# A fused spectral filter and gated GLU on one core: moments of six columns taken on ScalarE, transposed halves in PSUM banks of their own, first units of two weight slices

## Chip, core and metric

The kernel runs on one core of a Trainium2 chip. The metric is device time in microseconds (us). Engines: PE is TensorE (PEld its weight loads), DVE is VectorE, ACT is ScalarE, POOL is GpSimd, SP is SyncE, which issues most of the DMAs.

## What is computed

The input x has 2048 rows of 512 values in bf16. Each row is normalised over its 512 values. The normalised rows go two ways: through a 2-D real FFT, a product with a complex filter and the inverse FFT (part A), and through a gated GLU with 1792 hidden values (part B). The output is the sum of x and both parts.

```python
def _layernorm(x, axis=-1, eps=1e-5):
    m = jnp.mean(x, axis=axis, keepdims=True)
    v = jnp.var(x, axis=axis, keepdims=True)
    return (x - m) / jnp.sqrt(v + eps)
...
    X = rfft2(x) * (w_r + 1j * w_i); y = irfft2(X)            # A
...
    h = _gelu(x @ w_gate) * (x @ w_up); y = h @ w_down        # B
...
    return x + A(xn) + B(xn)          # xn = _layernorm(x)
```

## The kernel before

**Tiling.** The 2048 rows are cut into 16 groups that the code calls columns (c): row 16 p + c lies on partition p, column c. A column is a tile of 128 partitions by 512 values. The 512 values are four pieces of 128, numbered e. The 1792 hidden values are 14 slices of 128, numbered f; the weights Wg_sb and Wu_sb hold all slices in on-chip memory. Four columns form a block; there are four blocks, with transposed activations in the tiles xnT[0] to xnT[3].

**Stages.** For each column, VectorE takes mean and variance (bn_stats L396, bn_aggr L403), adds epsilon (L404), GpSimd raises to the power -0.5 (L406), and VectorE writes the normalised column xn (L412). Columns 0 to 3 are transposed by TensorE against an identity (L428) into PSUM and copied into xnT (L431): column 0 in two halves, the first copied by ScalarE and the second by VectorE, the others in one piece by ScalarE. Columns 4 to 15 are transposed by DMA (L437, issued by SP). The GLU (function glu) multiplies the transposed columns with slices of both weights (L502) into the PSUM tiles g_ps and u_ps, ScalarE applies gelu to g_ps (L519), and VectorE multiplies with u_ps into hT (L527). Two buffers each exist for g_ps and u_ps, so the matmuls of a unit wait for the gelu and the product of the unit two before. The list FIRST (L537) names the first units as (first column, number of columns, first slice, number of slices); then follow slices 6 to 13 for all four columns of block 0, then the other blocks.

The spectral part starts with folds of xn on VectorE (L555 to L567) and matmuls with the table RF_t (bp, L581); each of the four fold groups needs four normalised columns. Later stages (dp, ep, the filter, gp, yp) follow in the same style, and the last stage multiplies hT with w_down, adds the inverse transform in the same PSUM tile, adds x and stores.

**Loads.** x comes in five loads in this order of issue on SP, with the weight slices between them: column 0, column 1, columns 2 and 3, columns 4 to 7, columns 8 to 11; columns 12 to 15 and RF_t are issued later, behind the DMA transposes of columns 4 to 6.

**Order.** The order of instructions on each engine is not the order of the code. Every step is handed to a planner (class _Plan) with an engine, an estimated duration, dependencies, PSUM or work buffers, and a priority, mostly a due time. The planner runs a simple model (its own estimates for engines, DMA bandwidth and semaphore delay) and picks, whenever an engine is free in that model, the ready step with the lowest priority value. The order that comes out is written down and the engines run it as it stands. An engine's instructions therefore run in that order whether or not the model's times come true.

TensorE begins with ten matmuls on a constant tile (NWARM) and, behind column 0's transposes, four narrow ones (GAP).

Of the kernel before, what the change touches and what calls it, by code (L numbers as in the profile page):

```python
# [10 lines left out]
P = 128  # L11
BF16 = mybir.dt.bfloat16
# [206 lines left out]
def kernel(  # L219
# [43 lines left out]
    half = pc.tile([P, NC], F32, name="half")  # L263
    warm = pc.tile([P, D], BF16, name="warm")
    eps = pc.tile([P, 2], F32, name="eps")
    tiles = {}

    def cc(name):
# [43 lines left out]

    def load_x(c0, n, eng="SP", deps=()):
        q = nc.sync if eng == "SP" else nc.scalar
        o = load(n * P * D * 2, lambda: q.dma_start(out=x_t[:, c0:c0 + n], in_=x_v[:, c0:c0 + n]), deps, eng=eng)
        for c in range(c0, c0 + n):
            XD[c] = o

# [53 lines left out]
    o_mem = [add("POOL", 0.3, lambda: nc.gpsimd.memset(warm[:], 1.0), (), -20, lag=0.05),  # L372
             add("POOL", 0.2, lambda: nc.gpsimd.memset(half[:], -0.5), (), -15, lag=0.05)]  # L373
    wb = _Buf("S")
    NWARM, NGAP, GAP = 10, 1, 4

    def warm_mm(w):
        if "warm" not in tiles:
# [16 lines left out]
        tiles["st", c] = st  # L395
        V.bn_stats(out=st[:], in_=x_t[:, c])  # L396

    def layernorm(c0, n, due, after=(), halves=1):
        k = slice(c0, c0 + n)
        ag = []  # L400
        for c in range(c0, c0 + n):
            s = dve(0.6, lambda c=c: stats(c), [XD[c]] + list(after), due - 3.0 + 0.01 * (c - c0))
            ag.append(dve(0.15, lambda c=c: V.bn_aggr(out=mv[:, c], in_=tiles["st", c][:]), (s,), due - 3.2, ))  # L403
        e = dve(0.07, lambda: V.tensor_scalar(  # L404
            out=ve[:, k], in0=mv[:, k, 1], scalar1=EPS, scalar2=None, op0=ALU.add), ag, due - 5)
        r = add("POOL", 0.55, lambda: nc.gpsimd.tensor_tensor(  # L406
            out=rstd[:, k], in0=ve[:, k], in1=half[:, k], op=ALU.pow), (e, o_mem[1]), due - 5, lag=0.1)
        for c in range(c0, c0 + n):
            XN[c] = []
            for h in range(halves):  # L410
                d = slice(h * D // halves, (h + 1) * D // halves)
                XN[c].append(dve(0.04 + 0.29 / halves, lambda c=c, d=d: V.tensor_scalar(  # L412
                    out=xn[:, c, d], in0=x_t[:, c, d], scalar1=mv[:, c, 0:1], scalar2=rstd[:, c:c + 1],
                    op0=ALU.subtract, op1=ALU.mult), (r,), due - 2.5))
        return ag

    def pe_transpose(c, due):
        XT[c] = []
        b = _Buf("S")
        n = len(XN[c])  # L420
        for h in range(n):
            es = range(h * NE // n, (h + 1) * NE // n)

            def mm(h=h, es=es):
                if h == 0:
                    psum(f"tp.{c}", [P, NE, P], BF16)
                for e in es:
                    nc.tensor.transpose(tiles[f"tp.{c}"][:, e], xn[:, c, e * P:(e + 1) * P], ident)  # L428

            def ev(es=es, eng=(nc.scalar.copy, V.tensor_copy)[h]):  # L430
                eng(out=xnT[c // 4][:, es[0]:es[-1] + 1, c % 4], in_=tiles[f"tp.{c}"][:, es[0]:es[-1] + 1])  # L431

            o = pe(0.24 / n, mm, (XN[c][h], d_ident), due - 2, new=(b,) if h == 0 else (), use=(b,))
            XT[c].append((act, dve)[h](0.1 + 0.35 / n, ev, (o,), due - 30, use=(b,)))

    def dma_transpose(c, due):
        XT[c] = [dma(320e3, lambda: nc.sync.dma_start_transpose(out=xnT[c // 4][:, :, c % 4], in_=xn[:, c]),  # L437
                    XN[c], due - 30, lag=1.0)]

    first = layernorm(0, 1, -28, (), 2)  # L440
    layernorm(1, 1, -25, first)
    for c in range(4):
        if c == 2:
            layernorm(2, 2, -22, XT[0])
        pe_transpose(c, -28 + 3 * c)
        if c < NGAP:
            dummies(GAP, -29.9 + 3 * c, XN[c], P)
    for c0, n, due in ((4, 2, 14), (6, 2, 16), (8, 4, 24), (12, 4, 32)):
        layernorm(c0, n, due)
        for c in range(c0, c0 + n):  # L450
            dma_transpose(c, due)
        if c0 == 6:
            d_rf = load(P * NC * P * 2, lambda: nc.sync.dma_start(
                out=RF_t[:], in_=rf_d.rearrange("p (c k) -> p c k", c=NC)), XN[7])
            load_x(12, 4, deps=XN[7])
# [30 lines left out]
    def glu(c0, n, f0, nf=1, extra=()):  # L486
        sb, o, w = c0 // 4, (c0 % 4) * P, n * P
        gb, ub, eb = _Buf("G"), _Buf("U"), _Buf("ge")
        key = f"{c0}.{n}.{f0}"
        t = now[0]  # L490
        dur = NE * (w / 2400.0 + 0.0024)
        now[0] += 2 * dur * nf + 0.2

        def rhs(e):
            return xnT[sb][:, e, c0 % 4:c0 % 4 + n, :].rearrange("p c q -> p (c q)")

        def mm(nm, W, tag, a, b):
            if a == 0:
                psum(f"{nm}.{key}", [P, D], tag=tag)
            for f in range(a, b):  # L500
                for e in range(NE):
                    nc.tensor.matmul(tiles[f"{nm}.{key}"][:, f * w:f * w + w], lhsT=W[:, e, (f0 + f) * P:(f0 + f + 1) * P],  # L502
                                     rhs=rhs(e), start=(f + e == 0), stop=(f == nf - 1 and e == NE - 1),
                                     skip_group_check=nf > 1)

        g = [o for c in range(c0, c0 + n) for o in XT[c]]
        step = min(nf, 2)
        us = []
        for a in range(0, nf, step):
            deps = g[-1:] if a else g  # L510
            new = [([], []), ([gb], [ub])][a == 0]
            g = [pe(step * dur, lambda a=a: mm("g_ps", Wg_sb, "G", a, a + step), deps + [WD[f0 + a][0]], t,
                    new=new[0], use=(gb,))]
            us = [pe(step * dur, lambda a=a: mm("u_ps", Wu_sb, "U", a, a + step), us + g + [WD[f0 + a][1]], t,
                     new=new[1], use=(ub,))]

        def ge():
            e = work(f"ge.{key}", [P, D], "ge")
            nc.scalar.activation(out=e[:, 0:nf * w], in_=tiles[f"g_ps.{key}"][:, 0:nf * w], func=AF.Gelu_apprx_tanh)  # L519

        a = act(0.1 + nf * w / 1200.0, ge, g, t - 40, new=(eb,), use=(gb,))

        def mul():
            out = hslot(sb, f0)[:, o:o + w]
            if nf > 1:
                out = tiles["hT", sb][:, f0:f0 + nf, o:o + w]
            V.tensor_tensor(out=out, in0=tiles[f"u_ps.{key}"][:, 0:nf * w].rearrange("p (f w) -> p f w", w=w)  # L527
                            if nf > 1 else tiles[f"u_ps.{key}"][:, 0:w],
                            in1=tiles[f"ge.{key}"][:, 0:nf * w].rearrange("p (f w) -> p f w", w=w)
                            if nf > 1 else tiles[f"ge.{key}"][:, 0:w], op=ALU.mult)  # L530

        h = dve(0.08 + nf * w / 960.0, mul, us + [a] + list(extra), t - 40, use=(ub, eb))
        for c in range(c0, c0 + n):
            HT.setdefault(c, []).append(h)
        return h

    FIRST = [(0, 1, 0, 4), (1, 1, 0, 4), (0, 2, 4, 2), (2, 2, 0, 2), (2, 2, 2, 2), (2, 2, 4, 2)]  # L537
    for c, n, f, nf in FIRST + [(0, 4, f, 1) for f in range(6, NFC)]:
        glu(c, n, f, nf)

# [386 lines left out]
```

## Time and profile before

| | us |
|---|---|
| median of 8 runs | 179.66 (179.37 to 180.81) |
| the profiled execution | 179.58 |
| its span | 177.8 |
| PE busy | 172.9 (97%) |
| DVE busy | 118.3 (67%) |
| ACT busy | 87.5 (49%) |
| POOL busy | 18.5 (10%) |
| gelu, 128 x 512 (L519), mean of one | 0.598 |
| product into hT, 128 x 512 (L527), mean of one | 0.686 |
| bn_stats, 128 x 512 (L396), mean of one | 0.678 |

The span is the time from the first to the last instruction in the trace; the time of an execution also has what lies around it, here 1.8 us. Every time below is counted from the start of the span. PE's busy time counts pipelined matmuls whose ends are modelled, so a rate is read from the distance between the starts of two groups rather than from their durations. In a row of a timeline the brackets say how long the engine was idle before the instruction and what released it.

### The profile page before, as it was taken

How to read it: one execution, taken by the hardware profiler on the slowest of the kernel's cores; microseconds unless marked ns; L12 is line 12 of the kernel's file. 1: busy time of each engine (PE TensorE's matmuls, PEld its weight loads, DVE VectorE, ACT ScalarE, POOL GpSimd, SP SyncE). 2: the span in 40 equal slices, each digit the busy share in tenths (PEclk: the TensorE clock that was granted, in tenths of full speed). 3: DMA queues.
4: the chain of work that ended last, by engine and by line, in shares of the span. 5: the costliest groups of instructions: out<-in, count | busy, mean ns of one | idle time of the engine just before them, and what ended most of it. 6: DMA issues, size and time to landing. Idle time of an engine off the chain costs nothing.

```text
span 177.8 us, 3041 instructions
## 1 busy us (share of the span) xinstructions
PE 172.9 (97%) x1100; PEld 92.6 (52%) x1100; DVE 118.3 (67%) x266; ACT 87.5 (49%) x158; POOL 18.5 (10%) x33
## 2 busy tenths in 40 slices
PE   6899999999999999999999999999999999999993
PEld 2598545545554554554555455555445444544463
DVE  2759999999537995889999885336442541632522
ACT  3262427456789737999998855453111211211100
POOL 3212128743300000000000000000000000000000
PEclk9999999999999999999999999999999999999999
DMA  5999379899498001402211122000222221322212
GB/s 135 311 354 366 84 238 116 219 293 174 76 346 262 0 0 24 97 2 59 61 42 39 41 59 49 16 0 0 79 72 73 76 89 59 92 78 70 71 47 59
DMA packets 23182, 19.24 MB, mean 108 GB/s; under 512 B 8512, under 2 KB 21824, under 8 KB 23168
## 3 DMA queue, kind: packets, MB, share of 16 engines
q1 hardware_dynamic: 22176, 17.57, 35.9%
q0 software_dynamic: 320, 1.19, 3.1%
q10 hardware_dynamic: 672, 0.30, 0.6%
q8 instruction: 8, 0.13, 0.3%
q14 instruction: 6, 0.05, 0.1%
HBM read 13.28 MB, written 2.10 MB: 86 GB/s over the span
## 4 chain that ended last, share of the span: by engine, by line
PE 87%; ACT 3%; DMA 3%; DVE 3%; SPq 1%; issue 1%; DVEq 0%
PE u_ps L502 25%; PE g_ps L502 24%; DMA Wu_sb<-in_B_w_up_dram 3%; ACT E L652 2%; PE yp L818 2%; PE bp L581 2%; PE gp L767 2%; PE yp__2078 L872 2%; PE yp__2052 L872 2%; PE yp__2025 L872 2%; PE yp__1994 L872 2%; PE yp__1967 L872 2%; PE yp__1878 L872 2%; PE yp__1851 L872 2%; PE yp__1820 L872 2%; PE yp__1793 L872 2%
## 5 line engine op out<-in xcount | busy, mean ns | idle before, releaser
L502 PE MATMUL g_ps<-xnT,Wg_sb 128*128 128x512 bf16 (+2 forms) x264 | 58.1, 347 | 0.4 <-ACT xnT L431 0.2
L502 PE MATMUL u_ps<-xnT,Wu_sb 128*128 128x512 bf16 (+2 forms) x264 | 57.9, 347 | 0.3 <-DMA Wu_sb<-in_B_w_up_dram 0.3
L527 DVE TENSOR_TENSOR hT<-u_ps,ge 128x512 bf16<-128x512 f32 x56 | 38.4, 686 | 17.7 <-PE u_ps L502 15.1
L519 ACT ACTIVATE ge<-g_ps 128x512 bf16<-128x512 f32 x56 | 33.5, 598 | 30.9 <-PE g_ps L502 28.2
L502 PEld LDWEIGHTS <-Wu_sb 128*128 128x128 bf16 x264 | 24.3, 98 | 22.5 <-DMA Wu_sb<-in_B_w_up_dram 0.5
L502 PEld LDWEIGHTS <-Wg_sb 128*128 128x128 bf16 x264 | 24.1, 98 | 21.2 <-issue 0.4
L872 PEld LDWEIGHTS <-hT 128*128 128x128 bf16 x252 | 23.0, 98 | 21.9
L824 ACT CAST yf<-yp 128x512 bf16<-128x512 f32 x16 | 9.3, 586 | 37.6 <-PE yp L818 37.6
L652 ACT CAST E<-ep 64x512 bf16<-64x512 f32 x32 | 18.5, 579 | 1.1 <-PE ep L646 0.7
L396 DVE BATCH_NORM_STATS2 st<-x_t 128x6 f32<-128x512 bf16 x16 | 10.5, 678 | 4.7 <-DMA x_t<-in_A_x_dram 4.6
L629 ACT CAST ds<-dp 128x512 bf16<-128x512 f32 x16 | 8.8, 589 | 1.1 <-PE dp L624 1.0
L773 ACT CAST Gs<-gp 128x512 bf16<-128x512 f32 x16 | 8.6, 593 | 1.0 <-PE gp L767 1.0
L406 POOL TENSOR_TENSOR rstd<-ve,half 128x2 f32<-128x2 f32 (+2 forms) x7 | 6.6, 947 | 22.1 <-DVE ve L404 22.1
L585 ACT CAST Bs<-bp 128x512 bf16<-128x512 f32 x16 | 8.3, 603 | 0.5 <-PE bp L581 0.5
L818 PEld LDWEIGHTS <-Gs 128*128 128x128 bf16 x64 | 4.8, 98 | 3.5
L412 DVE TENSOR_SCALAR xn<-x_t,mv,rstd 128x512 bf16<-128x512 bf16 (+1 forms) x17 | 6.1, 400 | 0.3 <-POOL rstd L406 0.3
L818 PE MATMUL yp<-CT,Gs 128*128 128x128 bf16 x64 | 6.0, 219 | 0.0
L380 PE MATMUL warm<-warm 128*128 128x512 bf16 (+1 forms) x14 | 4.7, 502 | 1.3 <-POOL half L373 1.3
L683 DVE TENSOR_TENSOR m<-X,TW 128x1024 bf16<-128x1024 bf16 x8 | 5.5, 693 | 0.2
L624 PEld LDWEIGHTS <-Bs 128*128 128x128 bf16 x64 | 4.4, 98 | 2.4
L689 DVE TENSOR_TENSOR m<-X,TW 128x1024 bf16<-128x1024 bf16 x8 | 5.5, 685 | 0.0
L646 PE MATMUL ep<-ds,CT 128*128 128x512 bf16 x16 | 5.4, 379 | 0.0
(103 smaller groups left out, 168.8 us busy)
## 6 DMA issues: line engine op xcount, KB each, us to landing
y<-in_A_x_dram SPq DMA_DIRECT2D x16, 128.0 KB, 2.2
F<-F SPq DMA_DIRECT2D x32, 64.0 KB, 2.0
out_dram<-y SPq DMA_DIRECT2D x15, 128.0 KB, 1.7
Wd_sb<-in_B_w_down_dram SPq DMA_DIRECT2D x2, 896.0 KB, 7.3
x_t<-in_A_x_dram SPq DMA_DIRECT2D x3, 512.0 KB, 6.8
Wg_sb<-in_B_w_gate_dram SPq DMA_DIRECT2D x2, 512.0 KB, 6.8
Wu_sb<-in_B_w_up_dram SPq DMA_DIRECT2D x2, 512.0 KB, 9.1
Wg_sb<-in_B_w_gate_dram SPq DMA_DIRECT2D x3, 256.0 KB, 4.5
```

The lines of the kernel that those rows point to most:

```text
L396: V.bn_stats(out=st[:], in_=x_t[:, c])
L406: r = add("POOL", 0.55, lambda: nc.gpsimd.tensor_tensor(out=rstd[:, k], in0=ve[:, k], in1=half[:, k], op=ALU.pow), (e, o_mem[1]), due - 5, ...
L502: nc.tensor.matmul(tiles[f"{nm}.{key}"][:, f * w:f * w + w], lhsT=W[:, e, (f0 + f) * P:(f0 + f + 1) * P], rhs=rhs(e), start=(f + e == 0), ...
L519: nc.scalar.activation(out=e[:, 0:nf * w], in_=tiles[f"g_ps.{key}"][:, 0:nf * w], func=AF.Gelu_apprx_tanh)
L527: V.tensor_tensor(out=out, in0=tiles[f"u_ps.{key}"][:, 0:nf * w].rearrange("p (f w) -> p f w", w=w) if nf > 1 else tiles[f"u_ps.{key}"][:, ...
L585: nc.scalar.copy(out=o, in_=tiles[f"bp.{cg}.{q}"][:].rearrange("p c (r g a) -> p (c r) g a", r=2, a=4))
L629: nc.scalar.copy(out=ds[:].rearrange("p (s k t) -> p s k t", s=2, t=2), in_=tiles[f"dp.{G}"][:].rearrange("p s t k -> p s k t"))
L652: nc.scalar.copy(out=tiles[f"E.{g}"][64 * h:64 * h + 64, r], in_=tiles[f"ep.{g}.{h}"][64 * r:64 * r + 64])
L773: nc.scalar.copy(out=o, in_=tiles[f"gp.{g}.{h}"][:].rearrange("p q (n a) -> p (q n) a", a=4))
L818: nc.tensor.matmul(yp[:, q], lhsT=tiles["G"][:, q, c], rhs=IQ[q], start=(q == 0), stop=(q == 3), skip_group_check=True)
L824: nc.scalar.copy(out=tiles[f"yf.{c // 2}"][:, c % 2], in_=tiles[f"yp.{c}"][:])
L872: nc.tensor.matmul(y[:, s], lhsT=tiles[sb, f][:, cl * P:(cl + 1) * P], rhs=Wd_sb[:, f, s], start=(f == 0), stop=False)
```

## The change

ScalarE takes the moments of columns 1, 3, 5, 7, 9 and 11 with two ACTIVATE instructions that accumulate along the row: Identity with scale -1/512 gives the negative mean, and Square with that as bias gives 512 times the variance. Their elementwise outputs go to xn and are overwritten. For these columns VectorE scales and adds epsilon in one instruction and normalises with an addition in place of a subtraction. Epsilon is now added for each column by itself; the power still runs for a group of columns. Columns 2 and 3 become groups of their own.

Column 1 is also normalised and transposed in two halves, and each half has its own PSUM tile. Inside a GLU unit the matmuls with the first two pieces e come before those with the last two. FIRST starts with two slices for column 0 and two for column 1, and slices 2 and 3 are done for both columns together. Two of the four narrow fillers go. The planner is told half the bytes for the loads of columns 0 and 1, and columns 4 to 15 are made to depend on column 3's normalised values (in the planner alone). All of this is run through the planner again, so the order on every engine changes.

```diff
--- before.py
+++ after.py
@@ -263,6 +263,7 @@
     half = pc.tile([P, NC], F32, name="half")
     warm = pc.tile([P, D], BF16, name="warm")
     eps = pc.tile([P, 2], F32, name="eps")
+    sm = pc.tile([P, 2, NC], F32, name="sm")
     tiles = {}
 
     def cc(name):
@@ -312,7 +313,7 @@
 
     def load_x(c0, n, eng="SP", deps=()):
         q = nc.sync if eng == "SP" else nc.scalar
-        o = load(n * P * D * 2, lambda: q.dma_start(out=x_t[:, c0:c0 + n], in_=x_v[:, c0:c0 + n]), deps, eng=eng)
+        o = load(n * P * D * (2 if c0 > 1 else 1), lambda: q.dma_start(out=x_t[:, c0:c0 + n], in_=x_v[:, c0:c0 + n]), deps, eng=eng)
         for c in range(c0, c0 + n):
             XD[c] = o
 
@@ -372,7 +373,7 @@
     o_mem = [add("POOL", 0.3, lambda: nc.gpsimd.memset(warm[:], 1.0), (), -20, lag=0.05),
              add("POOL", 0.2, lambda: nc.gpsimd.memset(half[:], -0.5), (), -15, lag=0.05)]
     wb = _Buf("S")
-    NWARM, NGAP, GAP = 10, 1, 4
+    NWARM, NGAP, GAP = 10, 1, 2
 
     def warm_mm(w):
         if "warm" not in tiles:
@@ -395,58 +396,70 @@
         tiles["st", c] = st
         V.bn_stats(out=st[:], in_=x_t[:, c])
 
-    def layernorm(c0, n, due, after=(), halves=1):
+    def layernorm(c0, n, due, after=(), halves=1, acts=(), after2=()):
         k = slice(c0, c0 + n)
-        ag = []
+        es = []
         for c in range(c0, c0 + n):
-            s = dve(0.6, lambda c=c: stats(c), [XD[c]] + list(after), due - 3.0 + 0.01 * (c - c0))
-            ag.append(dve(0.15, lambda c=c: V.bn_aggr(out=mv[:, c], in_=tiles["st", c][:]), (s,), due - 3.2, ))
-        e = dve(0.07, lambda: V.tensor_scalar(
-            out=ve[:, k], in0=mv[:, k, 1], scalar1=EPS, scalar2=None, op0=ALU.add), ag, due - 5)
+            if c in acts:
+                m = act(0.62, lambda c=c: moment(c, AF.Identity, scale=-1.0 / D, accum_out=sm[:, 0, c:c + 1]),
+                        [XD[c]] + list(after), due - 30)
+                q = act(0.72, lambda c=c: moment(c, AF.Square, bias=sm[:, 0, c:c + 1], scale=1.0,
+                                                 accum_out=sm[:, 1, c:c + 1]), [m] + list(after2), due - 30)
+                es.append(dve(0.07, lambda c=c: V.tensor_scalar(
+                    out=ve[:, c:c + 1], in0=sm[:, 1, c:c + 1], scalar1=1.0 / D, scalar2=EPS, op0=ALU.mult, op1=ALU.add),
+                    (q,), due - 9))
+            else:
+                s = dve(0.6, lambda c=c: stats(c), [XD[c]] + list(after), due - 3.0 + 0.01 * (c - c0))
+                a = dve(0.15, lambda c=c: V.bn_aggr(out=mv[:, c], in_=tiles["st", c][:]), (s,), due - 3.2)
+                es.append(dve(0.07, lambda c=c: V.tensor_scalar(
+                    out=ve[:, c:c + 1], in0=mv[:, c, 1:2], scalar1=EPS, scalar2=None, op0=ALU.add), (a,), due - 5))
         r = add("POOL", 0.55, lambda: nc.gpsimd.tensor_tensor(
-            out=rstd[:, k], in0=ve[:, k], in1=half[:, k], op=ALU.pow), (e, o_mem[1]), due - 5, lag=0.1)
+            out=rstd[:, k], in0=ve[:, k], in1=half[:, k], op=ALU.pow), es + [o_mem[1]], due - 5, lag=0.1)
         for c in range(c0, c0 + n):
             XN[c] = []
+            mean, op = (sm[:, 0, c:c + 1], ALU.add) if c in acts else (mv[:, c, 0:1], ALU.subtract)
             for h in range(halves):
                 d = slice(h * D // halves, (h + 1) * D // halves)
-                XN[c].append(dve(0.04 + 0.29 / halves, lambda c=c, d=d: V.tensor_scalar(
-                    out=xn[:, c, d], in0=x_t[:, c, d], scalar1=mv[:, c, 0:1], scalar2=rstd[:, c:c + 1],
-                    op0=ALU.subtract, op1=ALU.mult), (r,), due - 2.5))
-        return ag
+                XN[c].append(dve(0.04 + 0.29 / halves, lambda c=c, d=d, mean=mean, op=op: V.tensor_scalar(
+                    out=xn[:, c, d], in0=x_t[:, c, d], scalar1=mean, scalar2=rstd[:, c:c + 1],
+                    op0=op, op1=ALU.mult), (r,), due - 2.5))
+
+    def moment(c, func, **kw):
+        nc.scalar.activation(out=xn[:, c], in_=x_t[:, c], func=func, **kw)
 
     def pe_transpose(c, due):
         XT[c] = []
-        b = _Buf("S")
         n = len(XN[c])
         for h in range(n):
+            b = _Buf("S")
             es = range(h * NE // n, (h + 1) * NE // n)
 
             def mm(h=h, es=es):
-                if h == 0:
-                    psum(f"tp.{c}", [P, NE, P], BF16)
+                psum(f"tp.{c}.{h}", [P, NE, P], BF16)
                 for e in es:
-                    nc.tensor.transpose(tiles[f"tp.{c}"][:, e], xn[:, c, e * P:(e + 1) * P], ident)
-
-            def ev(es=es, eng=(nc.scalar.copy, V.tensor_copy)[h]):
-                eng(out=xnT[c // 4][:, es[0]:es[-1] + 1, c % 4], in_=tiles[f"tp.{c}"][:, es[0]:es[-1] + 1])
-
-            o = pe(0.24 / n, mm, (XN[c][h], d_ident), due - 2, new=(b,) if h == 0 else (), use=(b,))
+                    nc.tensor.transpose(tiles[f"tp.{c}.{h}"][:, e], xn[:, c, e * P:(e + 1) * P], ident)
+
+            def ev(h=h, es=es, eng=(nc.scalar.copy, V.tensor_copy)[h]):
+                eng(out=xnT[c // 4][:, es[0]:es[-1] + 1, c % 4], in_=tiles[f"tp.{c}.{h}"][:, es[0]:es[-1] + 1])
+
+            o = pe(0.24 / n, mm, (XN[c][h], d_ident), due - 2, new=(b,))
             XT[c].append((act, dve)[h](0.1 + 0.35 / n, ev, (o,), due - 30, use=(b,)))
 
     def dma_transpose(c, due):
         XT[c] = [dma(320e3, lambda: nc.sync.dma_start_transpose(out=xnT[c // 4][:, :, c % 4], in_=xn[:, c]),
                     XN[c], due - 30, lag=1.0)]
 
-    first = layernorm(0, 1, -28, (), 2)
-    layernorm(1, 1, -25, first)
-    for c in range(4):
-        if c == 2:
-            layernorm(2, 2, -22, XT[0])
-        pe_transpose(c, -28 + 3 * c)
-        if c < NGAP:
-            dummies(GAP, -29.9 + 3 * c, XN[c], P)
+    layernorm(0, 1, -28, (), 2)
+    layernorm(1, 1, -25, (), 2, (1,))
+    pe_transpose(0, -28)
+    dummies(GAP, -29.9, XN[0], P)
+    pe_transpose(1, -25)
+    layernorm(2, 1, -22, XN[1])
+    pe_transpose(2, -22)
+    layernorm(3, 1, -19, XT[0], 1, (3,), XT[1])
+    pe_transpose(3, -19)
     for c0, n, due in ((4, 2, 14), (6, 2, 16), (8, 4, 24), (12, 4, 32)):
-        layernorm(c0, n, due)
+        layernorm(c0, n, due, XN[3], 1, (5, 7, 9, 11))
         for c in range(c0, c0 + n):
             dma_transpose(c, due)
         if c0 == 6:
@@ -497,11 +510,10 @@
         def mm(nm, W, tag, a, b):
             if a == 0:
                 psum(f"{nm}.{key}", [P, D], tag=tag)
-            for f in range(a, b):
-                for e in range(NE):
-                    nc.tensor.matmul(tiles[f"{nm}.{key}"][:, f * w:f * w + w], lhsT=W[:, e, (f0 + f) * P:(f0 + f + 1) * P],
-                                     rhs=rhs(e), start=(f + e == 0), stop=(f == nf - 1 and e == NE - 1),
-                                     skip_group_check=nf > 1)
+            for f, e in sorted(((f, e) for f in range(a, b) for e in range(NE)), key=lambda k: (k[1] // 2, k)):
+                nc.tensor.matmul(tiles[f"{nm}.{key}"][:, f * w:f * w + w], lhsT=W[:, e, (f0 + f) * P:(f0 + f + 1) * P],
+                                 rhs=rhs(e), start=(f + e == 0), stop=(f == nf - 1 and e == NE - 1),
+                                 skip_group_check=nf > 1)
 
         g = [o for c in range(c0, c0 + n) for o in XT[c]]
         step = min(nf, 2)
@@ -534,7 +546,7 @@
             HT.setdefault(c, []).append(h)
         return h
 
-    FIRST = [(0, 1, 0, 4), (1, 1, 0, 4), (0, 2, 4, 2), (2, 2, 0, 2), (2, 2, 2, 2), (2, 2, 4, 2)]
+    FIRST = [(0, 1, 0, 2), (1, 1, 0, 2), (0, 2, 2, 2), (0, 2, 4, 2), (2, 2, 0, 2), (2, 2, 2, 2), (2, 2, 4, 2)]
     for c, n, f, nf in FIRST + [(0, 4, f, 1) for f in range(6, NFC)]:
         glu(c, n, f, nf)
```

## Prediction

> **What bounds the kernel now.** I began with the busy line of the page, then the waits of the matmul queue.
>
> ```profile
> PE 172.9 (97%) x1100; PEld 92.6 (52%) x1100; DVE 118.3 (67%) x266; ACT 87.5 (49%) x158; POOL 18.5 (10%) x33
> ...
> PE warm L380 <- POOL half L373: 1.3, 1, 1.3
> PE u_ps L502 <- DMA Wu_sb<-in_B_w_up_dram: 0.3, 1, 0.3
> PE g_ps L502 <- ACT xnT L431: 0.2, 1, 0.2
> ```
>
> TensorE is busy for 172.9 of 177.8 us, and its three named waits all fall before 9.1 us. The table of stretches gives 40.00 busy in 100 to 140 us and 39.88 in 60 to 100. So from 9.03 us on, TensorE is the bound, and whatever the change gives or takes must show as an idle stretch of that engine: a little can be won before 9 us, anything can be lost after. The next rows are timelines (start, duration, engine, line, operation), of PE, ACT and DVE in turn.
>
> ```profile
> 9.03 0.62 PE L502 MATMUL u_ps<-xnT,Wu_sb 128*128 128x128 bf16 x8 [0.28 <-DMA Wu_sb<-in_B_w_up_dram]
> ...
> 11.72 1.04 PE L502 MATMUL g_ps<-xnT,Wg_sb 128*128 128x256 bf16 x8
> 12.59 1.04 PE L502 MATMUL u_ps<-xnT,Wu_sb 128*128 128x256 bf16 x8
> 13.46 1.04 PE L502 MATMUL g_ps<-xnT,Wg_sb 128*128 128x256 bf16 x8
> ...
> 27.34 1.06 PE L581 MATMUL bp<-RF_t,xf 128*128 128x128 bf16 x16
> ...
> 11.70 1.07 ACT L431 COPY xnT<-tp 128x512 bf16<-128x512 bf16 x2
> 12.79 0.60 ACT L519 ACTIVATE ge<-g_ps 128x512 bf16<-128x512 f32 x1
> ...
> 7.24 1.29 DVE L396 BATCH_NORM_STATS2 st<-x_t 128x6 f32<-128x512 bf16 x2
> ...
> 12.42 0.69 DVE L396 BATCH_NORM_STATS2 st<-x_t 128x6 f32<-128x512 bf16 x1 [1.32 <-DMA x_t<-in_A_x_dram]
> 13.03 0.67 DVE L527 TENSOR_TENSOR hT<-u_ps,ge 128x512 bf16<-128x512 f32 x1
> ```
>
> Starts tell the rate better than durations: eight matmuls of 128 columns take 0.45 us, eight of 256 take 0.875, four of 512 take 0.865, sixteen bp 0.89. The matmul at 13.46 is the first to use columns 2 and 3; ScalarE copied their transposes at 11.70, so they had some 0.7 us in hand. VectorE sat idle for 1.32 us until columns 4 to 7 of x landed at 12.42. ScalarE has no wait for a load of x at all. That is what changes.
>
> **Part 1, TensorE's own work.** Two of four filler matmuls go: 2 x 0.055 = 0.11. Eight groups of 0.45 (3.58 us) become four of 0.45 and two of 0.875 (3.54). Together 0.15 us less. Sorting matmuls by half of the contraction moves none across a group.
>
> **Part 2, the first 11.7 us.** Now the first copy of column 0 at 6.08 waits for all four transposes (the last ends at 6.05), and VectorE's copy waits for ScalarE's. With a bank each, ScalarE can copy once two transposes are done, at 5.82, and the first matmul can go at 6.2 instead of 6.51. Against that, the second half of column 0 stands on VectorE behind column 1's variance, which waits for ScalarE's two passes: x1 landed at 1.19 + 2.9 = 4.1, Identity to 4.7, Square to 5.45, so that half starts at 5.6 rather than 5.4.
>
> Then the built order of ScalarE matters. After the copy of column 0 it has Identity of column 3, then the first gelu, then column 1's copy. Columns 2 and 3 land at 2.13 + 5.1 = 7.23 us, as VectorE's row at 7.24 agrees. Identity at 7.26, one pitch of 0.49 (the second of the two copies at 11.70 adds 0.48), a gelu of 256 elements some 0.30, and column 1's copy runs 8.05 to 8.42. Its matmuls start at 8.48 and go through: u 8.93, the 256-wide group 9.38 and 10.25, transposes of 2 and 3 at 11.13, next group at 11.57 instead of 11.72. Weights are in time (the slice that arrives at 9.03 is now wanted at 10.25). Column 3's Square ends at 9.05, its normalised column at 10.65, before 11.13. So the bank split and the reordered start, which could save up to 1.3 us if nothing waited, give only the 0.15 of part 1.
>
> **Part 3, the wait that is added.** The next Identity on ScalarE is column 5's, which needs the same load for which VectorE waited until 12.42. Behind it in ScalarE's queue stand **the two copies of columns 2 and 3**, then Square of column 5 and the gelu of the running group. Now these copies start at 11.70; in the change they start one pitch after 12.42: 12.42 + 0.49 + 0.48 + 0.59 = 13.98 for the end of the second, and 0.06 to the matmul (6.45 to 6.51 in the first copy): **14.04 against 13.46**, when TensorE alone would be ready at 11.57 + 1.75 = 13.32. Loss 0.58 after the gain of 0.15 is used up.
>
> An accumulating ACTIVATE has no row here. Lower bound: the gelu's 0.60 and pitch 0.49. Upper: no overlap and 0.2 more, 0.8, which makes it 14.35. I take the gelu's row. The Trainium skill ("ScalarE: Activation LUTs", section What ACT_TABLE_LOAD costs) gives 186 ns + 0.833 ns an element, 93 ns more for a per-partition bias, 93 ns of overlap: 0.61 and 0.71, pitch 0.52, so by the rule 14.07. The same page (Rules for kernel authors) says additions and multiplications belong on VectorE, not ScalarE. Rows: statistics of a column cost VectorE 0.69 + 0.18, and here two passes on ScalarE, 0.60 + 0.71. As throughput this is hidden: ScalarE is busy 1.96 of 4 us from 12 to 16, and 12 passes add some 7 us over 4 to 21 us. By the rule alone one would book ScalarE's longer work, by the rows nothing; my loss comes from where the passes stand in the queue.
>
> **Part 4, from 14 to 24 us.** Does the crowded ScalarE hold TensorE again? Gelu of (columns 0-1, slices 4-5) ends at 15.1, wanted at 15.8; of (columns 2-3, slices 0-1) 16.1, wanted 17.5. Column 9's Identity waits for columns 8 to 11 (8.38 + 9.0 = 17.38), with the gelu behind it ending at 18.5, wanted at 19.3. VectorE's product of (columns 0-1, slices 4-5) ends at 16.4, wanted at 16.7, the tightest. VectorE loses six statistics and aggregations (about 6 x 0.7 by pitch) and gains nine small variance instructions (9 x 0.08). POOL gets one more power, 0.6, beside TensorE. Nothing stalls, by 0.3 us at least.
>
> **Part 5, the fold matmuls.** The built order puts the first bp group two units earlier: after three units at 256 columns and three at 512, so at 14.04 + 6 x 0.875 + 6 x 0.865 = 24.48 (the same sum with ten groups gives 27.36 now, as the trace has it). It needs RF_t, behind three transposes on SP:
>
> ```profile
> 17.98 4.35 SPq L437 DMA_TRANSPOSE xnT<-xn  x3
> 22.38 0.57 SPq L453 DMA_DIRECT2D RF_t<-spec_rf  x1
> ...
> DMA to landing us min/median/max: 4.2/4.2/4.2
> ```
>
> (The last line is RF_t's alone.) It landed at 26.6, 0.75 us before its use. In the change column 4 is normalised by 16.8 (after the product at 15.75 to 16.4); the three transposes issue for 1.3, 1.2 and 1.2 us at 16.85, 18.25 and 19.5; RF_t issues at 20.75 and lands at **24.95**. TensorE waits **0.47**. Bounds: none, if the load takes 3.7; 1.0, if column 4 or 6 slips by half a us.
>
> **Part 6, the rest.** The order of later groups differs, but each load and spectral step moves up some 3 us with its consumer. The second fold group, due near 30.2, has its operand at 28.7; the first gp group, due at 72.7, its F near 68. I cost this at nothing; the cover is VectorE's lighter load, and if it fails, one late product or F costs 0.3 to 1.
>
> **Sum.** 0.58 + 0.47 = 1.05 on the profiled execution's 179.58 us (span 177.8 and 1.8 around it): 180.63; the median of the runs shown, 179.66, is within 0.1. **Forecast 180.6 us.**
>
> **The clock.** Removing fillers could hurt otherwise. The ten warm-up matmuls of 512 columns follow each other at 0.43 us, later ones at 0.216. "TensorE: Matmul & The Clock Gate" (Part 1) says half rate returns after an idle window of about 3.4 us. My longest idle stretch is 0.8 (7.7 to 8.5), so by the rule nothing; yet little work lies between 5.5 and 9 us. If a window fell to half rate, 3.4 us would do 1.7 us of work, less 0.7 hidden before 14.04: 1.0 more, 181.6.
>
> **Rivals.**
> - Only ScalarE's wait counts, RF_t is in time: 180.16. For: 0.47 is small beside the spread of load times (x between 2.5 and 9.0 us). Against: the transposes' issue chain is firm. 0.25.
> - Both waits and a third loss (dear accumulation, a late product, the half clock): 181.1 to 182. For: thin covers in part 4. 0.18.
> - Faster or no change: column 5's pass does not hold the copies. This decides if columns 4 to 7 land before 13.32 - 0.06 - 0.59 - 0.48 - 0.49 = 11.70 us; then the 0.15 of part 1 stays, 179.43, and, should columns 2 and 3 also land early, up to 1.3, 178.3. Against: loads keep their order, and VectorE's row puts the landing at 12.42. RF_t would have to be early as well. 0.10, about half beyond 0.3%.
> - The forecast, both waits: 0.47, 180.3 to 181.0.
>
> **Chances and range.** A measurement of this kernel tells 0.3%, 0.54 us, from no change, so the edge is 180.2. Slower takes the forecast, the third-loss case and a third or so of the first rival: 0.74. The rest of that rival and half the fast case: within, 0.21. Faster 0.05. Range 179.9 to 181.6: from a cheap first wait to the half clock.
>
> **What would show it.** In the profile after: Identity of column 5 on ScalarE ending an idle stretch near 12.4 with a DMA of x as releaser; the two copies after it; TensorE waiting 0.6 to 0.8 us on ScalarE just before 14; a wait of bp on RF_t's load near 24.5. It is wrong if the copies run before 12, if TensorE has no wait after 9 us, or if the loss appears after 30 us.

## The result, and the profile after

| | before | after |
|---|---|---|
| median of the runs beside one another, us | 179.58 (179.11 to 180.81, 57 runs) | 180.30 (179.84 to 180.95, 20 runs) |
| ratio, with its 95% interval | | 1.0038 (1.0028 to 1.0048) |
| the profiled execution, us | 179.58 | 180.5 |
| its span, us | 177.8 | 178.7 |
| start of the first GLU matmul, us | 6.51 | 6.50 |
| start of the last matmul, us | 174.89 | 175.80 |

The change makes the kernel 0.38% slower, 0.7 us in the medians and 0.9 us in the two profiled executions. The page of the changed kernel has this busy line, and its waits of the matmul queue are these (total, times, longest):

```profile
PE 173.2 (97%) x1082; PEld 92.8 (52%) x1082; DVE 116.2 (65%) x266; ACT 95.5 (53%) x183; POOL 18.6 (10%) x34
...
PE warm L381 <- POOL half L374: 1.3, 1, 1.3
PE g_ps L514 <- ACT xnT L443: 1.1, 2, 0.6
PE bp L593 <- DMA RF_t<-spec_rf: 0.3, 1, 0.3
```

ScalarE is busy for 8.0 us more and VectorE for 2.1 us less; neither bounds anything, and neither number tells where the time went. The waits do: those of the kernel before on Wu_sb and on the first copy are gone, and three others stand in their place. TensorE's timeline has them in place:

```profile
8.76 0.61 PE L514 MATMUL g_ps<-xnT,Wg_sb 128*128 128x128 bf16 x8 [0.63 <-ACT xnT L443]
...
11.84 1.04 PE L514 MATMUL g_ps<-xnT,Wg_sb 128*128 128x256 bf16 x8
12.72 1.04 PE L514 MATMUL u_ps<-xnT,Wu_sb 128*128 128x256 bf16 x8
14.20 1.03 PE L514 MATMUL g_ps<-xnT,Wg_sb 128*128 128x256 bf16 x8 [0.45 <-ACT xnT L443]
...
25.09 1.05 PE L593 MATMUL bp<-RF_t,xf 128*128 128x128 bf16 x16 [0.31 <-DMA RF_t<-spec_rf]
```

A bracket is shorter than what is lost, since the row before it lasts 1.03 to 1.04 us where the next group can start after 0.865 to 0.875: by starts, 14.20 stands 0.61 behind 12.72 + 0.875, and 25.09 stands 0.47 behind the group before it (23.75) + 0.865. ScalarE's queue shows why columns 2 and 3 came late:

```profile
7.45 0.63 ACT L428 ACTIVATE xn<-x_t 128x512 bf16<-128x512 bf16 x1 [1.04 <-DMA x_t<-in_A_x_dram]
7.99 0.18 ACT L428 ACTIVATION_READ_ACCUMULATOR xn<-x_t 128x1 f32 x1
8.08 0.36 ACT L531 ACTIVATE ge<-g_ps 128x256 bf16<-128x256 f32 x1
8.35 0.36 ACT L443 COPY xnT<-tp 128x256 bf16<-128x256 bf16 x1
...
12.47 0.63 ACT L428 ACTIVATE xn<-x_t 128x512 bf16<-128x512 bf16 x1 [1.15 <-DMA x_t<-in_A_x_dram]
13.00 0.19 ACT L428 ACTIVATION_READ_ACCUMULATOR xn<-x_t 128x1 f32 x1
13.10 1.05 ACT L443 COPY xnT<-tp 128x512 bf16<-128x512 bf16 x2
```

Read the first and the fifth row by their brackets: ScalarE stood still for 1.04 and 1.15 us, because the instruction at the head of its queue (Identity of column 3, then of column 5) waited for a load of x. The copies TensorE wants are two to three rows further down. Column 1's transposes were in PSUM by 7.7 us and its copy starts at 8.35; those of columns 2 and 3 were there by 12.0 and their copies start at 13.10. And SP's queue, with the landing of RF_t:

```profile
16.84 3.92 SPq L449 DMA_TRANSPOSE xnT<-xn  x3
20.81 0.57 SPq L466 DMA_DIRECT2D RF_t<-spec_rf  x1
...
DMA to landing us min/median/max: 4.2/4.2/4.2
```

RF_t lands at 20.81 + 4.2 = 25.0 and its matmul goes at 25.09.

**The balance.** The matmul on columns 2 and 3 starts 0.74 us later than before (14.20 against 13.46), bp loses 0.47, and the last matmul is only 0.91 later. So 0.30 us came back after 25 us. Nearly all of it is a stall that the kernel before had near 76 us and the changed one doesn't (39.88 and 40.00 us busy of 40 from 60 to 100 us):

```profile
75.45 1.12 PE L767 MATMUL gp<-CT,F 128*128 128x128 bf16 x12
76.40 1.03 PE L502 MATMUL u_ps<-xnT,Wu_sb 128*128 128x512 bf16 x4
```

Twelve matmuls of 128 columns take 0.67 us and here take 0.95, so 0.28 is lost between the eighth (75.84) and the ninth (76.18); the idle of 0.12 is what is left of it by durations. The profile names no releaser. All five profiles without the four later columns on ScalarE (before, e4, e8, e10, e11) have this stall, and the nine with them don't, so it is a small gain of the change.

### The profile page after: what moved, and what is told of

Its sections match the earlier page's. It is cut to its first block, busy times and chain, and to the rows that moved or that the text cites. A ratio compares the mean times of both kernels' runs of the same rounds, so it can differ in the third digit from the quotient of the medians.

```text
span 178.7 us, 3030 instructions
## 1 busy us (share of the span) xinstructions
PE 173.2 (97%) x1082; PEld 92.8 (52%) x1082; DVE 116.2 (65%) x266; ACT 95.5 (53%) x183; POOL 18.6 (10%) x34
## 4 chain that ended last, share of the span: by engine, by line
PE 87%; DMA 6%; SPq 3%; DVE 1%; ACT 1%; issue 1%; ACTq 0%
PE g_ps L514 24%; PE u_ps L514 24%; DMA x_t<-in_A_x_dram 4%; DMA RF_t<-spec_rf 2%; PE bp L593 2%; PE gp L779 2%; PE dp L636 2%; PE yp L830 2%; PE ep L658 2%; SPq L326 2%; PE yp__2074 L884 2%; PE yp__2048 L884 2%; PE yp__2021 L884 2%; PE yp__1990 L884 2%; PE yp__1963 L884 2%; PE yp__1874 L884 2%
## 5 line engine op out<-in xcount | busy, mean ns | idle before, releaser
L539 DVE TENSOR_TENSOR hT<-u_ps,ge 128x512 bf16<-128x512 f32 (+1 forms) x57 | 38.7, 680 | 20.7 <-PE u_ps L514 16.3
L531 ACT ACTIVATE ge<-g_ps 128x512 bf16<-128x512 f32 (+1 forms) x57 | 33.7, 591 | 22.4 <-PE g_ps L514 21.9
L397 DVE BATCH_NORM_STATS2 st<-x_t 128x6 f32<-128x512 bf16 x10 | 6.7, 679 | 4.7 <-DMA x_t<-in_A_x_dram 4.6
L416 POOL TENSOR_TENSOR rstd<-ve,half 128x1 f32<-128x1 f32 (+2 forms) x8 | 6.6, 831 | 18.8 <-DVE ve L414 11.6
L428 ACT ACTIVATE xn<-x_t 128x512 bf16<-128x512 bf16 x6 | 3.8, 628 | 3.4 <-DMA x_t<-in_A_x_dram 3.4
L779 PEld LDWEIGHTS <-F 128*128 128x128 bf16 x64 | 4.2, 98 | 1.9
```

The source lines that it names most:

```text
L779: nc.tensor.matmul(gp[:, q], lhsT=F[:, h, q % 2, q // 2::2], rhs=cc("M" if 2 * g + h else "M0"), start=(q == 0), stop=(q == 3), skip_group ...
```

## The experiments

**The theory.** All of the loss comes from giving ScalarE the moments of the four later columns 5, 7, 9 and 11. Column 5's Identity waits for a load at the head of an in-order queue, and the PSUM copies behind it come late. And the planner, run with these columns on ScalarE, puts the first bp group two units earlier, due at 24.62 us in place of 27.34; RF_t, behind three transposes, is issued earlier than before as well, but only by 1.57 us (20.81 against 22.38). **Rivals**: the added work itself, the banks, or the new first units cost the time; or only one of the two waits counts. The runs came in three batches, each on another chip and with runs of the kernel before beside it. A ratio compares within its batch, and medians of different batches (before: 179.41, 179.54, 179.73) are not to be subtracted. The middle columns are read from each profiled execution: when VectorE began on column 0, the first GLU matmul, the last matmul.

| run | median, us | ratio (95%) | col. 0 | first | last |
|---|---|---|---|---|---|
| before | 179.58 | | 3.23 | 6.51 | 174.89 |
| after | 180.30 | 1.0038 (1.0028 to 1.0048) | 3.15 | 6.50 | 175.80 |
| e1_copies_first | 181.24 | 1.0097 (1.0065 to 1.0130) | 3.20 | 6.49 | 175.62 |
| e2_rf_early | 179.67 | 1.0016 (1.0000 to 1.0032) | 3.74 | 6.76 | 175.30 |
| e3_both | 180.01 | 1.0024 (1.0012 to 1.0036) | 3.19 | 6.47 | 175.41 |
| e4_vector_stats | 179.45 | 1.0008 (0.9995 to 1.0021) | 3.31 | 6.32 | 174.70 |
| e5_swap_only | 180.01 | 1.0018 (0.9996 to 1.0039) | 4.03 | 7.16 | 175.09 |
| e6_swap_rf | 179.67 | 0.9994 (0.9978 to 1.0010) | 3.84 | 6.86 | 175.34 |
| e7_all_moves | 179.43 | 0.9994 (0.9973 to 1.0015) | 4.26 | 7.29 | 175.04 |
| e8_vector_stats_early | 179.52 | 0.9991 (0.9970 to 1.0012) | 3.78 | 6.91 | 174.70 |
| e9_four_alone | 181.01 | 1.0073 (1.0057 to 1.0089) | 3.17 | 6.90 | 176.29 |
| e10_banks_alone | 179.49 | 0.9998 (0.9986 to 1.0010) | 3.13 | 6.41 | 174.70 |
| e11_first_alone | 179.90 | 1.0016 (1.0003 to 1.0029) | 3.14 | 6.44 | 174.92 |
| e12_all_moves_again | 179.18 | 0.9973 (0.9960 to 0.9986) | 3.66 | 6.79 | 174.38 |

### The four columns taken out: e4

```diff
-        layernorm(c0, n, due, XN[3], 1, (5, 7, 9, 11))
+        layernorm(c0, n, due, XN[3])
```

> The changed kernel, with the moments of columns 5, 7, 9 and 11 back on VectorE (columns 1 and 3 stay on ScalarE). Queue theory: ScalarE meets no load of columns 4 to 11, the copies run near 11.8, the matmul at 13.6, RF_t is again in time: about 179.6. Rival (the early part, columns 1 and 3 on ScalarE with the split banks, is what costs): stays near 180.3.

It measured 1.0008, no difference from before that can be told. Two rows of TensorE and one of ScalarE:

```profile
13.03 1.04 PE L514 MATMUL g_ps<-xnT,Wg_sb 128*128 128x256 bf16 x8
...
27.12 1.05 PE L593 MATMUL bp<-RF_t,xf 128*128 128x128 bf16 x16
...
11.26 1.07 ACT L443 COPY xnT<-tp 128x512 bf16<-128x512 bf16 x2 [0.50 <-PE tp L440]
```

The copies wait for the transposes alone, not for a load, and the matmul at 13.03 follows the group before it with no wait. bp stands behind ten groups again. It has no bracket, but by starts 0.21 us is lost there (27.12 against 26.04 + 0.865), because RF_t took 5.2 us to land in this profile. So the first wait is gone and less than half of the second is left, with columns 1 and 3, the banks and the first units still as the change has them.

### Each part alone: e9, e10, e11

e9 is the kernel before with this call, and the changed kernel's layernorm to serve it:

```diff
-        layernorm(c0, n, due)
+        layernorm(c0, n, due, XN[3], 1, (5, 7, 9, 11))
```

> The kernel before with the moments of columns 5, 7, 9 and 11 alone on ScalarE; column 1 and 3, the PSUM banks and the first units of the weight slices stay as they were. Theory (all of the loss is in these four columns): TensorE waits for the PSUM copies of columns 2 and 3 behind column 5's Identity, and for RF_t at bp: 180.2 to 180.5 us. Rival (the rest of the change is what makes the waits bite): 179.5.

1.0073, 1.3 us, slower than the whole change and than I expected. In TensorE's and SP's rows:

```profile
14.00 1.03 PE L515 MATMUL g_ps<-xnT,Wg_sb 128*128 128x256 bf16 x8 [0.46 <-ACT xnT L444]
...
25.57 1.05 PE L594 MATMUL bp<-RF_t,xf 128*128 128x128 bf16 x16 [0.99 <-DMA RF_t<-spec_rf]
...
21.28 0.57 SPq L466 DMA_DIRECT2D RF_t<-spec_rf  x1
```

The first wait is that of the changed kernel. RF_t is issued 0.47 us later than there (21.28 against 20.81): column 4 is normalised at 16.89 in place of 16.40, behind a product in VectorE's queue. So bp, due at 23.55 + 0.865 = 24.42, loses 1.15. With the 0.54 by which 14.00 is later than 13.46, less the 0.28 of the stall near 76 us, which this kernel doesn't have either, this is the 1.40 by which the last matmul is late. My edit also dropped an order between columns 0 and 1 on VectorE, so the first GLU matmul came at 6.90 although column 0 was there at 3.17; ScalarE's copies of columns 2 and 3, which end at 13.95 because Identity waited for its load until 12.27, swallow that. The rival is out: the four columns alone make both waits.

e10 gives each half of a transposed column its own bank, in the kernel before:

```diff
-        b = _Buf("S")
...
+            b = _Buf("S")
...
-                if h == 0:
-                    psum(f"tp.{c}", [P, NE, P], BF16)
+                psum(f"tp.{c}.{h}", [P, NE, P], BF16)
```

> The kernel before with the two halves of a transposed column in PSUM banks of their own, nothing else. In the kernel before, the VectorE copy of column 0 stands at 6.49 us against the ScalarE copy at 6.08. Theory: the two copies no longer wait for one another, the first matmul starts up to 0.4 us earlier, and most of that is lost again at the loads behind it: 179.3 to 179.5. Rival (a shared bank costs nothing here): the kernel before, 179.5 to 179.6.

0.9998. VectorE's copy of column 0 waits for ScalarE's before, and for the transposes alone here (the first two rows); the next groups then wait for weights:

```profile
6.49 0.29 DVE L431 COPY xnT<-tp 128x256 bf16<-128x256 bf16 x1 [0.72 <-ACT xnT L431]
...
6.25 0.29 DVE L430 COPY xnT<-tp 128x256 bf16<-128x256 bf16 x1 [0.32 <-PE tp L427]
...
7.95 0.62 PE L501 MATMUL g_ps<-xnT,Wg_sb 128*128 128x128 bf16 x8 [0.19 <-DMA Wg_sb<-in_B_w_gate_dram]
8.85 0.62 PE L501 MATMUL u_ps<-xnT,Wu_sb 128*128 128x128 bf16 x8 [0.28 <-DMA Wu_sb<-in_B_w_up_dram]
```

From the first transpose to the first GLU matmul it is now 0.74 us (5.67 to 6.41) where it was 1.00 (5.51 to 6.51). So the shared bank did cost 0.26 us there. Column 1 landed later in this profile and took 0.16 of it, since VectorE takes column 1's bn_stats ahead of normalising column 0; at the end nothing is left that can be measured.

e11 takes the new first units alone:

```diff
-    FIRST = [(0, 1, 0, 4), (1, 1, 0, 4), (0, 2, 4, 2), (2, 2, 0, 2), ...
+    FIRST = [(0, 1, 0, 2), (1, 1, 0, 2), (0, 2, 2, 2), (0, 2, 4, 2), (2, 2, 0, 2), ...
```

> The kernel before with the first units of matmuls over two weight slices where they were over four, nothing else. Theory (step 1 of the prediction): TensorE's own work falls by 0.15 us, but column 1's groups come 0.9 us earlier than its transposes are ready, so TensorE waits there: 179.5 to 179.9, with a wait of 0.3 to 0.9 us on the copy of column 1 or on column 2 and 3's transposes. Rival (two slices let TensorE start as early and lose nothing): 179.4.

1.0016 (0.3 us), and the expected wait is there, behind column 1's single copy:

```profile
8.60 0.61 PE L502 MATMUL g_ps<-xnT,Wg_sb 128*128 128x128 bf16 x8 [0.67 <-ACT xnT L431]
```

This is a second way to the wait at 8.76 in the changed kernel: shorter first units want column 1 earlier than it is ready.

### One cause at a time, planned anew: e1, e2, e3

e1 tells the planner that the moments of later columns depend on the copies of columns 2 and 3; e2 makes RF_t's load depend on column 4 in place of column 7, so that SP issues it ahead of the transposes; e3 does both.

```diff
+        layernorm(c0, n, due, XN[3], 1, (5, 7, 9, 11), (), XT[2] + XT[3])   # e1
...
-                out=RF_t[:], in_=rf_d.rearrange("p (c k) -> p c k", c=NC)), XN[7])
+                out=RF_t[:], in_=rf_d.rearrange("p (c k) -> p c k", c=NC)), XN[4])
```

> The changed kernel, with column 5's and later moments on ScalarE ordered behind the PSUM copies of columns 2 and 3; the same instructions otherwise. Queue theory (the copies stand behind a pass that waits for the load of columns 4 to 7): the copies run at about 11.8, the first matmul on columns 2 and 3 starts at 13.6 instead of 14.20 (where TensorE is free), and RF_t, which lands near 25.05, is in time for a fold group now due near 25.7. Both waits go, 0.6 + 0.3: about 179.6, the same as before. Rival (ScalarE is simply too loaded by twelve passes and their accumulator reads): the load is the same, so 180.3 stays.

e1 missed by 1.6 us. The copies do run at 11.29 and the matmul on columns 2 and 3 starts at 13.06 with no wait. But the planner, run again, also put column 9's Identity ahead of a gelu and ahead of column 7's Square:

```profile
16.39 0.63 ACT L428 ACTIVATE xn<-x_t 128x512 bf16<-128x512 bf16 x1 [1.05 <-DMA x_t<-in_A_x_dram]
...
22.16 0.57 SPq L466 DMA_DIRECT2D RF_t<-spec_rf  x1
...
26.64 1.05 PE L593 MATMUL bp<-RF_t,xf 128*128 128x128 bf16 x16 [0.95 <-DMA RF_t<-spec_rf]
```

It is the same fault in another place: ScalarE stands still for 1.05 us at a load, column 7's variance is late, with it the normalised pair 6 and 7, the third transpose and RF_t. This is not all of RF_t's delay of 1.35 us: the transposes begin 0.86 later than in the change (17.70 against 16.84), because VectorE's new order has column 5's variance at 15.87 in place of 14.99. The profiled execution (180.35) is near the fastest of e1's six; what the slower ones lost besides isn't seen.

> The changed kernel, with RF_t's load issued ahead of the DMA transposes instead of behind three of them. Theory: bp's wait of 0.31 us goes and the wait of 0.45 us on ScalarE near 14.2 stays, so 180.0. Rival (RF_t only takes up slack that another late operand would cost): a new wait near 25 us and 180.3.

> Both edits of the two runs before it. Theory: no wait of TensorE after 9 us; 1.05 us of stall less in the profile than the changed kernel less some 0.15 for TensorE's own readiness at 13.6: 179.5 to 179.7. If the two waits hid one another, only about 179.9.

e2 came to 1.0016, some 0.4 us below the change by the ratios, whose intervals just overlap. The wait at 14.16 stays, and bp has none:

```profile
14.16 1.03 PE L514 MATMUL g_ps<-xnT,Wg_sb 128*128 128x256 bf16 x8 [0.76 <-ACT xnT L443]
...
24.58 0.61 PE L593 MATMUL bp<-RF_t,xf 128*128 128x128 bf16 x8
```

Starts agree with bp at its due time: 14.16 + 6 x 0.875 + 6 x 0.865 = 24.60. The last matmul is 0.50 earlier than in the change. So RF_t's wait is worth some 0.4 to 0.5 by itself. e3 missed (1.0024): both waits were gone, but in the new order TensorE waited for VectorE at 16.20 (0.34) and for a folded operand at 30.12 (0.36). From here on I moved single instructions in the finished order and planned nothing anew.

### One instruction moved at a time: e5, e6, e7, e12

```diff
+    def behind(o, other):
+        order.remove(o)
+        order.insert(order.index(other) + 1, o)
+
+    behind(MO[5], XT[3][0])        # e5: column 5's Identity behind the copies of columns 2 and 3
```

> The changed kernel with one instruction moved in its finished order: column 5's Identity stands on ScalarE behind the PSUM copies of columns 2 and 3 instead of ahead of them; nothing is planned anew. Theory (a queue of waits): the matmul on columns 2 and 3 starts at about 13.1 to 13.6 us (14.20 in the changed kernel) with little or no wait, but RF_t still lands at about 25.05 us, so TensorE, earlier by what it gained, waits so much longer at bp (about 0.8 us in place of 0.31). The first wait is swallowed by the second: about 180.3 us, span 178.6. Rival (the wait behind Identity is worth its 0.6 us by itself): 179.7 us, span 178.1.

In TensorE's, SP's and VectorE's rows:

```profile
13.34 1.04 PE L516 MATMUL g_ps<-xnT,Wg_sb 128*128 128x256 bf16 x8
...
24.37 0.83 PE L595 MATMUL bp<-RF_t,xf 128*128 128x128 bf16 x12 [0.42 <-DMA RF_t<-spec_rf]
...
20.33 0.57 SPq L468 DMA_DIRECT2D RF_t<-spec_rf  x1
...
12.00 0.69 DVE L397 BATCH_NORM_STATS2 st<-x_t 128x6 f32<-128x512 bf16 x1 [1.10 <-DMA x_t<-in_A_x_dram]
```

The first wait is gone with one move. The time falls between theory and rival, 1.0018, but its interval reaches over both. In the profile bp starts 0.72 us earlier than in the change, and this isn't the move's doing. Columns 4 to 7 landed at 12.00 here and at 12.47 there; VectorE's row, full from then on, stands that much earlier, so the transposes start at 16.37 in place of 16.84 and RF_t is issued at 20.33; it then landed in 4.0 us in place of 4.2. Taken back by these two (an estimate: 24.37 + 0.48 + 0.2), bp stands at 25.05, within 0.04 of the change. So this profile fits the theory, that the second wait swallows the first, and the rival isn't borne out.

e6 adds e2's line to e5.

> As the run with the one swap, and RF_t's load issued behind column 4 instead of column 7, so that it stands on SP ahead of the transposes. Theory: both waits of the changed kernel are gone; what is left are short waits of TensorE on VectorE between 15 and 24 us, since its products stand behind bn_stats and folds that wait for loads. About 179.6 us, span 178.0. If the two waits were all that the change lost, it would be 179.3.

0.9994: level with before, as expected; the interval doesn't part the 179.6 of the theory from the 179.3 of two waits alone. TensorE's and VectorE's rows show what comes next:

```profile
16.82 1.03 PE L516 MATMUL u_ps<-xnT,Wu_sb 128*128 128x256 bf16 x8 [0.74 <-DVE ve L416]
...
16.09 0.68 DVE L541 TENSOR_TENSOR hT<-u_ps,ge 128x512 bf16<-128x512 f32 x1
```

The u group needs the buffer that the product at 16.09 frees at 16.77, and the product stands in VectorE's queue behind column 4's bn_stats (12.84, after a wait for the load) and two folds. (The bracket names the small instruction that ends next; the end that fits is the product's.) This is the product that the prediction called the tightest. How much it holds depends on the load: in e5, where the load landed at 12.00, it runs from 15.25 to 15.93 and costs 0.03 us.

e7 moves the rest:

```diff
+    behind(MO[3], XT[1][0])
+    behind(ST[2], XT[1][1])
+    behind(ST[4], HT[0][1])
+    behind(FOLD[0][0], HT[0][2])
+    behind(FOLD[0][1], FOLD[0][0])
+    behind(MO[9], GE[2, 2])
```

> As the run before, and the other instructions that wait for loads ahead of work that TensorE wants are moved behind it too: column 3's Identity behind column 1's PSUM copy on ScalarE, column 2's bn_stats behind column 1's PSUM copy on VectorE, column 4's bn_stats and the fold of A behind products, column 9's Identity behind a gelu. Theory: no wait of TensorE is left after about 9 us, and the second group of matmuls starts at about 8.0 instead of 8.76: about 178.9 us, span 177.2, below both kernels. Rival (the loads, not the queues, set the start: the third group ends its cover and waits for the copies of columns 2 and 3 by what was gained): 179.5.

> The same kernel as the run with all moves, once more, since its profile fell on a late landing of column 0 (VectorE began at 4.26 us, 3.15 in the changed kernel), which hides any later wait. If the queues alone made the waits, a profile with an early landing shows TensorE without a wait after its first matmul, too, and 178.9 us. If the loads set the start, TensorE waits 0.3 to 0.7 us for columns 1, or 2 and 3, and the median is again 179.3 to 179.5 us.

e7 measured 0.9994 (0.9973 to 1.0015). This leaves out the 178.9 of the theory (0.9964 of that batch's 179.54) and agrees with the rival's 179.5. Its profile has no wait of TensorE behind the first GLU matmul, but column 0 had landed so late there (VectorE at 4.26) that a later wait could have been hidden. The same kernel again (e12, column 0 at 3.66) measured 0.9973 (0.9960 to 0.9986), 0.5 us below before. Its matmul queue has one wait, at the start, and TensorE's rows have no bracket:

```profile
PE warm L381 <- POOL half L374: 1.3, 1, 1.3
...
6.79 0.62 PE L516 MATMUL g_ps<-xnT,Wg_sb 128*128 128x128 bf16 x8
...
8.15 0.61 PE L516 MATMUL g_ps<-xnT,Wg_sb 128*128 128x128 bf16 x8
...
13.13 1.04 PE L516 MATMUL g_ps<-xnT,Wg_sb 128*128 128x256 bf16 x8
...
23.55 1.06 PE L597 MATMUL bp<-RF_t,xf 128*128 128x128 bf16 x16
```

Column 1's group starts at 8.15 (8.76 in the change), columns 2 and 3 at 13.13 (14.20), bp at 23.55 (25.09), with the same six columns on ScalarE. So it is the place of the passes, and of RF_t's load, in the queues, not their work, that cost the time. Between the two profiles of this one kernel, e7 has column 0 later by 0.60 us, the first GLU matmul by 0.50 and the last matmul by 0.66; that the first load sets the end once the queues are free agrees with this, but two profiles don't show it. One batch says faster than before, by 0.3%, and one can't tell, so a gain is likely and not certain; against the changed kernel it is 0.4 to 0.65% by the ratios.

### The start alone, on top of e4: e8

The first two moves of e7, added to e4.

> The changed kernel with columns 5, 7, 9 and 11 on VectorE again (179.45 us measured), and column 3's Identity behind column 1's PSUM copy on ScalarE, column 2's bn_stats behind column 1's PSUM copy on VectorE. Theory: the second group starts at about 8.0 us in place of 8.76, up to 0.4 us of that reach the end: 179.0 to 179.1 us. Rival (the third group waits for columns 2 and 3 whatever the second does): 179.45.

Column 1's group starts with no wait, 1.36 us after the first GLU matmul (8.27 after 6.91), where e4 has 1.88. The ratio of 0.9991 (0.9970 to 1.0012) doesn't tell 0.4 us from nothing. Left open.

## Why the prediction held, step by step

The forecast was 180.6 us, on the profiled execution; that took 180.5, and the median is 180.30. It came about in the way foretold, two waits of TensorE. That the profiled execution comes within 0.1 us of the sum is in part luck, since two errors cancel (part 6); the medians lost 0.72 of the 1.05 us. The corrections:

**Part 1 (TensorE's work, -0.15 us): too large.** The 0.11 of the two fillers could not come in: before, TensorE is idle behind them in any case, for 0.24 us until the copy lets it go on at 6.51. Only the 0.04 of the first units is left. e11 has these alone and lost more at a wait.

**Part 2 (the start gains only 0.15): right in mechanism, still too hopeful.** Column 1's group was put at 8.48 and came at 8.76. Columns 2 and 3 landed at 7.45, not 7.23, and Identity took 0.63 from its start to the start of the next instruction, not 0.49. So not even the 0.15 came in: the group at 11.84 is 0.12 later than before. Identity of column 3 is what blocked column 1's copy on ScalarE (7.45 to 8.35); e7, e8 and e12, which move it and column 2's bn_stats behind the copies, have no wait there.

The first GLU matmul didn't come at 6.2 either, but at 6.50. This isn't the bank split but TensorE's rate. In e2, e4, e6 and e7, which have the same start, TensorE is at its full rate by then and the matmul comes 3.01 to 3.03 us after column 0, which would be 6.2 here; in the changed kernel it comes 3.35 after. The first row is of the kernel before, the others are of the changed one:

```profile
5.88 0.39 PE L380 MATMUL warm<-warm 128*128 128x128 bf16 x4
...
6.29 0.42 PE L381 MATMUL warm<-warm 128*128 128x128 bf16 x2
6.50 0.90 PE L514 MATMUL g_ps<-xnT,Wg_sb 128*128 128x128 bf16 x8
7.25 0.43 PE L440 MATMUL tp<-CT,xn 128*128 128x128 bf16 x4
```

Matmuls of 128 columns follow each other at 0.107 us in the changed kernel until 7.0 (two fillers in 0.21 us, the first group in 0.75) and at 0.056 afterwards, as the four fillers of the kernel before do from 5.88 on. It cost nothing further on, since column 1's copy waited behind Identity in any case.

**Part 3 (Identity of column 5 holds the copies, 14.04): right, 14.20.** Landing at 12.47 (12.42 expected) and 0.63 in place of 0.49 make the difference. The Trainium skill's 0.52 between starts ("ScalarE: Activation LUTs", What ACT_TABLE_LOAD costs) agrees with the ACTIVATE itself, 12.47 to 13.00; what neither rule nor gelu row had is the read of the accumulator behind it. The 0.8 that I kept as the upper end was not needed. e5 shows the step alone: with this one instruction moved, the wait is gone.

**Part 4 (no further stall from 14 to 24 us): right for this kernel, and only because it was late.** The tightest product, put at 15.75 to 16.4, ran from 15.71 to 16.39. With the earlier waits taken away and the load at 12.84 (e6), it held TensorE for 0.74 us. The cover that I named as thin was in part the late TensorE itself.

**Part 5 (bp waits 0.47 for RF_t): right.** Issue 20.81 (20.75 expected), landing 25.0 (24.95), due 24.62 (24.48), loss 0.47 by starts.

**Part 6 (nothing later): off by 0.28 us in the kernel's favour**, the stall near 76 us in the balance above, which I had not seen in the kernel before. It more than cancels the 0.16 by which part 3 was too small: the sum said 1.05, the profiled execution has 0.92.

**The clock:** granted in full (1.00) in every stretch of the table of stretches, and yet matmul starts stood at half the later rate until 7.0 us, as in part 2. So the start is slow, not because a slow rate came back but because the warm-up's own lasted longer, and at no cost that reaches 14 us. This doesn't tell whether the missing fillers did it: the moved kernel, with the same two fillers, has the full rate from 4.6 us in e7 and still the slow one at 6.5 in e12. No stretch between two matmuls is longer than 1.4 us in any profile here, so what the prediction says of an idle window of 3.4 us is shown by no run. **Only ScalarE's wait:** out, RF_t was late for its matmul and its wait is worth about 0.4 by e2. **Faster, with early loads:** columns 4 to 7 would have had to land by 11.70; they came at 12.47 here and between 11.9 and 12.8 in all fourteen profiles. I didn't try loads in another order.

## What to carry to other kernels

Before work is given to an idle engine, list what stands behind it in that engine's queue, and place whatever waits for a load behind everything that TensorE already wants. An idle share says nothing about it: ScalarE was half idle, and one of its waits at a load still cost TensorE 0.6 us at the copies. The same holds for a load in SP's queue: RF_t behind three transposes cost 0.5 us as soon as its matmul was planned earlier. Moving seven instructions and this one load within their queues gave both back. When one wait is removed, look for the next before counting the gain, and don't let a planner reorder everything while a single cause is tested.

## What the hardware showed unexpectedly

- **An accumulating ACTIVATE is two instructions.** Behind each of the twelve stands an ACTIVATION_READ_ACCUMULATOR of 0.18 to 0.21 us that adds about 0.1 to the distance between starts (Identity 0.53 to its read, 0.63 to what follows). Square with a bias per partition takes 0.71 to 0.73 where Identity takes 0.63.
- **TensorE's slow first rate ends at different times.** In every profile the warm-up matmuls of 512 columns start at 1.34 us and stand 0.43 apart. The distance halves to 0.217 at 4.2 us in e4 and at 4.6 in e7, while in the changed kernel the slow rate lasts until 7.0 (0.107 between matmuls of 128 columns), with a granted clock of 1.00 in all three.
- **The first load lands within a spread of 1.1 us.** Column 0 is issued at 0.73 us in every profile, and VectorE begins on it between 3.13 and 4.26. In the second batch all four are at 3.78 or later, in the other runs at 3.74 or earlier. This is of the size of all that was to be told apart here, and why ratios within a batch and waits in the traces carry the argument, not single times.
